# Smaller tiles (44 rows for 60), a smaller first tile and an unaligned TensorE program in a channel-gate kernel

## The chip, the cores and the metric

One core of one Trainium2 chip. The metric is the device time of one execution in microseconds (us); lower is better.

## The reference

```python
def reference(x, w1d):                     # x: (1, 384, 384, 384) bf16, w1d: (1,) bf16
    B, H, W, C = x.shape
    g = jnp.einsum("bhwc->bc", x) / (H * W)     # mean of each channel over all pixels
    s = _sigmoid(g * w1d[0])                    # (the loop over k = 1 taps, shortened)
    return x * s[:, None, None, :]
```

The input is 113.25 MB and so is the output. The kernel treats x as 1152 rows: one row is 128 pixels, one on each of 128 partitions, of 384 channels (768 bytes on each partition).

## The kernel before

Read literally, the reference needs two passes over x: one for the mean and one for the product. The kernel makes a single pass by a guess. It computes the gate `s_early` from the first few rows only, multiplies every tile by it in place and stores the tile. Meanwhile TensorE sums all rows. At the end the true gate `s_true` is computed and compared bit by bit in bf16. If any channel differed, a second pass would redo everything. With this input the gates agree, so the second pass is only a flag that is read and found to be zero.

```python
FIRST, TILE, PART, SLOTS = 12, 60, 28, 4
...
def sum_others():
    def one(e, s):                                   # one tile, in slot s
        e.wait_ge(ready, 1).then_inc(ready, -1)
        for r, n in parts:                           # parts = (0, PART), (PART, TILE-PART)
            add_rows(e, 1, (slot(s) + r) * C, n, 0, False, False).then_inc(...)
    def emit(e):
        ...
        with e.Fori(0, rounds) as k:                 # TensorE's loop: one round is SLOTS tiles
            for s in range(some):
                one(e, s)
            if some < SLOTS:
                with e.If(k < rounds - 1):
                    for s in range(some, SLOTS):
                        one(e, s)
...
for k in range(n_tiles):
    if k >= SLOTS:
        j = k - SLOTS
        put(row0(j), slot(j), slot(j), TILE, parts)  # VectorE: two gates; ScalarE's queue: store
        if k < last:
            load(slot(k), TILE, row0(k))             # SyncE's queue: waits for that store
        else:
            for r, n in parts:                       # the last tile is loaded in two parts
                load(slot(k), TILE, row0(k), r, n)
    for r, n in parts:
        plan.relay(ready, "gpsimd", "tensor",        # tells TensorE that the tile has landed
                   rows(slot(k), TILE) if r == 0 else (), ...)
...
# the end: add the PSUM banks (VectorE), s_true (ScalarE), compare, reduce, flag (VectorE)
def second_pass(name, e):
    e.wait_ge(*checked)
    flag = e.value_load(redo[0:1, 0:1], min_val=0, max_val=1)
    with e.If(flag > 0):
        ...
@block.scalar
def _(e):
    plan.emit("scalar", e)
    second_pass("scalar", e)
    for token in plan.final:                         # all stores
        e.wait_ge(*token)
@block.tensor
def _(e):
    e.addr_align(256, max_nops=0)
    plan.emit("tensor", e)
```

A tile in slot `s` is loaded, summed, gated part by part, stored, and then the slot is loaded anew. The loop of TensorE is unrolled over four slots of 45 matmuls of 512 columns.

## Time and profile before

| | kernel before |
|---|---|
| time, median of 3 runs | 531.79 us (531.5 to 532.03) |
| span of the profiled run | 530.1 us |
| time per tile in mid-run (load + store of 11.80 MB) | 27.18 us, so 434 GB/s |
| last load landed, slowest DMA engine | 508.94 us |
| flag read by ScalarE | 526.81 us |
| last store landed: median of the 16 DMA engines / slowest one | 526.48 / 529.63 us |

The first view is the page of the kernel before: span, busy time of each engine, the DMA share in 40 slices (tenths, 9 is 90% or more), and the queues with packets, MB and share of the 16 engines' span.

```profile
span 530.1 us, 1079 instructions
...
PE 227.4 (43%) x857; PEld 0.2 (0%) x2; DVE 241.5 (46%) x57; ACT 2.7 (1%) x4; POOL 0.3 (0%) x6
...
DMA  8999999999999999999999999999999999999996
...
q10 hardware_dynamic: 3314, 121.90, 53.2%
q1 hardware_dynamic: 2880, 104.60, 45.9%
q8 instruction: 1, 0.02, 0.0%
q14 instruction: 2, 0.02, 0.0%
...
```

SyncE's queue q1 and ScalarE's queue q10 together fill 99.1% of the 16 engines' span, and no compute engine comes near (VectorE 46%, TensorE 43%). The line q8, of the kind "instruction", is a single packet of 16384 B, called the instruction fetch in this document. The trace's DMA records put it at 2.4 us, and it took 2.045 us. It is the only one of the run, though TensorE's loop goes through five rounds.

Two waits look large. The table of waits (engine and line, what was waited for, us in total, times, longest):

```profile
...
PE acc L236 <- PEq L275: 283.6, 18, 31.1
DVE arena L199 <- PE acc L236: 245.3, 16, 28.5
...
```

These are engines waiting for tiles that have yet to land. With the queues at 99.1% of the 16 DMA engines' span, none of this waiting lengthens the middle of the run.

Whether it stays full in the middle is read from the loads that SyncE issues (start, duration, count), in the timeline from 210 to 300 us:

```profile
...
213.45 81.87 SPq L109 DMA_DIRECT2D arena<-in_x_dram  x4
```

Four issues, the first start to the last end 81.87 us, one issue 0.33 us: three periods of 27.18 us. A data packet of 46080 B takes 1.702 us in the DMA records. A tile is 128 of them in and 128 out, so by even division 8 in and 8 out for each of 16 DMA engines, and 16 × 1.702 = 27.23 us, the period: the engines run without a gap.

So only start and end are left to gain. The end in the timeline (start us, duration, engine, line, operation, count, idle time before and its releaser):

```profile
...
508.96 6.56 DVE L199 TENSOR_TENSOR arena<-arena,s_early 128x12288 bf16<-128x12288 bf16 x1 [16.54 <-DMA arena<-in_x_dram]
509.08 12.30 PE L236 MATMUL acc<-arena,ones 128*128 128x512 bf16 x45 [31.13 <-PEq L275]
...
521.22 0.81 PE L236 MATMUL acc<-zeros,ones 128*128 128x512 bf16 x3
522.07 2.70 DVE L309 TENSOR_TENSOR total<-total,acc 128x384 f32<-128x384 f32 x6 [6.55 <-PE acc L236]
524.80 0.61 ACT L412 ACTIVATE s_true<-total,w_scaled 128x384 bf16<-128x384 f32 x1 [507.61 <-DVE total L309]
...
526.63 0.15 DVE L434 CAST redo<-wrong 128x1 int32<-128x1 f32 x1
```

The last load's slowest part lands at 508.94. Then two things race: the last gate and its store, and TensorE's sum of the whole last tile (13 us) with a chain of small steps to the flag. How the DMA drains, by stretch (window, its length, then busy time and instruction count of each engine, granted clock, DMA share, GB/s):

```profile
...
core 0: us, PE busy (x) PEld busy (x) DVE busy (x) ACT busy (x) POOL busy (x), PEclk, DMA share, GB/s
...
520.00:524.00 4.00, 2.03 (x10) 0.00 (x0) 1.79 (x5) 0.00 (x0) 0.00 (x0) 1.00 1.02 439
524.00:526.00 2.00, 0.00 (x0) 0.00 (x0) 1.28 (x3) 0.61 (x1) 0.00 (x0) 0.57 0.77 332
526.00:528.00 2.00, 0.00 (x0) 0.00 (x0) 0.71 (x3) 0.00 (x0) 0.00 (x0) 0.50 0.12 49
528.00:530.00 2.00, 0.00 (x0) 0.00 (x0) 0.00 (x0) 0.00 (x0) 0.00 (x0) 0.50 0.09 33
...
```

From 526 us on the DMA share is about a tenth, which is one or two of the 16 engines: 14 have finished by 527.05, and two land their part of the last store at 529.34 and 529.63. ScalarE's last store wait passes at 529.65 and the span ends 0.45 us later. The slowest DMA engine sets the end.

### The profile page before, as it was taken

To read this page: it belongs to the slowest core of one execution; us is meant where nothing else is said; L and a number is where in the kernel's file an instruction comes from. 1 tells how busy PE (TensorE), PEld (TensorE's weight loads), DVE (VectorE), ACT (ScalarE), POOL (GpSimd) and SP (SyncE) were. 2 spreads that over 40 slices of the span, in tenths; PEclk is the share of its full clock that TensorE was granted. 3 is DMA by queue.
4 is the path that set the end of the run, shared out by engine and by line. 5 is a ranking of instruction groups with operands and counts; after the bars stand their busy time and mean duration, and the time that the engine had idled before them with its cause. 6 is when DMAs were issued, how large, how long until landed. Compare 5 with 4: busy or idle time off the path is not lost. (4 is left out here: it accounts for less than half of the span.)

```text
span 530.1 us, 1079 instructions
## 1 busy us (share of the span) xinstructions
PE 227.4 (43%) x857; PEld 0.2 (0%) x2; DVE 241.5 (46%) x57; ACT 2.7 (1%) x4; POOL 0.3 (0%) x6
## 2 busy tenths in 40 slices
PE   2284971052434436262717080908080808070053
PEld 0000000000000000000000000000000000000000
DVE  0353997008080907172625353445344443538142
ACT  1000000000000000000000000000000000000000
POOL 0000000000000000000000000000000000000000
PEclk9786987568686958585858585859686868777567
DMA  8999999999999999999999999999999999999996
GB/s 361 445 445 404 408 445 438 421 431 435 445 428 428 431 435 445 431 424 435 435 445 431 424 428 442 445 428 428 428 442 445 424 431 424 445 420 458 418 421 299
DMA packets 6197, 226.53 MB, mean 427 GB/s; under 512 B 690, under 2 KB 690, under 8 KB 690
## 3 DMA queue, kind: packets, MB, share of 16 engines
q10 hardware_dynamic: 3314, 121.90, 53.2%
q1 hardware_dynamic: 2880, 104.60, 45.9%
q8 instruction: 1, 0.02, 0.0%
q14 instruction: 2, 0.02, 0.0%
HBM read 113.25 MB, written 113.25 MB: 427 GB/s over the span
## 5 line engine op out<-in xcount | busy, mean ns | idle before, releaser
L199 DVE TENSOR_TENSOR arena<-arena,s_early 128x10752 bf16<-128x10752 bf16 (+2 forms) x39 | 234.8, 6063 | 264.2 <-PE acc L236 245.3
L236 PE MATMUL acc<-arena,ones 128*128 128x512 bf16 x849 | 224.9, 429 | 285.0 <-PEq L275 283.6
L309 DVE TENSOR_TENSOR total<-total,acc 128x128 f32<-128x128 f32 (+2 forms) x11 | 4.5, 409 | 6.9 <-PE acc L236 6.5
L307 DVE COPY total<-acc 128x384 f32<-128x384 f32 x1 | 0.6, 558 | 11.4 <-PE acc L236 11.4
L234 PE MATMUL acc<-arena,ones 128*128 128x512 bf16 x1 | 0.6, 606 | 7.6 <-DMA arena<-in_x_dram 7.6
L412 ACT ACTIVATE s_true<-total,w_scaled 128x384 bf16<-128x384 f32 x1 | 0.6, 614 | 507.6 <-DVE total L309 507.6
L236 PE MATMUL acc<-zeros,ones 128*128 128x512 bf16 x6 | 2.3, 505 | 0.0
L338 ACT ACT_TABLE_LOAD x1 | 1.3, 1283 | 2.2 <-issue 2.2
L344 PE MATMUL w_all<-w_one,ones 1*128 1x1 bf16 x1 | 0.2, 158 | 2.0 <-DMA w_one<-in_w1d_dram 2.0
L420 DVE TENSOR_TENSOR total<-s_true,s_early 128x384 f32<-128x384 uint16 x1 | 0.6, 559 | 0.7 <-ACT s_true L412 0.7
L353 DVE TENSOR_SCALAR w_scaled<-w_all 128x1 f32<-128x1 f32 x2 | 0.2, 154 | 1.3 <-PE w_all L344 1.3
L375 ACT ACTIVATE s_early<-total,w_scaled 128x384 bf16<-128x384 f32 x1 | 0.6, 614 | 12.9 <-DVE total L309 12.9
L428 DVE TENSOR_REDUCE wrong<-total 128x1 f32<-128x384 f32 x1 | 0.6, 553 | 0.0
L362 DVE MEMSET ones<- 128x128 bf16 x1 | 0.2, 165 | 0.8 <-PEq L512 0.8
L338 ACT ACTIVATE warm<-warm 128x1 f32<-128x1 f32 x1 | 0.2, 203 | 0.0
L434 DVE CAST redo<-wrong 128x1 int32<-128x1 f32 x1 | 0.2, 153 | 0.0
L234 PEld LDWEIGHTS acc<-arena,ones 128*128 128x128 bf16 x1 | 0.1, 105 | 7.7 <-DMA arena<-in_x_dram 7.7
L344 PEld LDWEIGHTS w_all<-w_one,ones 1*128 1x128 bf16 x1 | 0.1, 101 | 2.0 <-issue 2.0
L512 POOL MEMSET const-bfloat16-1.0<- 128x1 bf16 x1 | 0.1, 101 | 0.0
L512 POOL MEMSET const-uint8-127<- 128x1 uint8 x1 | 0.1, 101 | 0.0
L361 POOL MEMSET zeros<- 128x2 bf16 x1 | 0.1, 99 | 0.0
L360 POOL MEMSET warm<- 128x1 f32 x1 | 0.1, 98 | 0.3 <-POOLq L512 0.3
(2 smaller groups left out, 0.2 us busy)
## 6 DMA issues: line engine op xcount, KB each, us to landing
out_dram<-arena ACTq DMA_DIRECT2D x18, 5760.0 KB, 53.5
arena<-in_x_dram SPq DMA_DIRECT2D x16, 5760.0 KB, 35.4
arena<-in_x_dram SPq DMA_DIRECT2D x2, 3072.0 KB, 37.3
arena<-in_x_dram ACTq DMA_DIRECT2D x1, 5760.0 KB, 45.1
out_dram<-arena ACTq DMA_DIRECT2D x1, 3072.0 KB, 14.1
arena<-in_x_dram ACTq DMA_DIRECT2D x1, 2688.0 KB, 18.7
arena<-in_x_dram SPq DMA_DIRECT2D x1, 2688.0 KB, 28.5
out_dram<-arena ACTq DMA_DIRECT2D x1, 2688.0 KB, 29.9
```

The source lines that it names most:

```text
L199: return lambda e: e.tensor_tensor(to_v, v, s_b, ALU.mult)
L234: loaded.append(e.matmul(bank, weights, moving, start=start, stop=stop))
L236: return e.add_instruction(mybir.InstMatmult(name=nc.get_next_instruction_name(), engine=mybir.EngineType.PE, ins=[e.lower_ap(moving), e.l ...
L307: emit = lambda e, part=part, of=of: e.tensor_copy(part, of)
L309: emit = lambda e, part=part, of=of: e.tensor_tensor(part, part, of, ALU.add)
L338: lambda e: e.activation(warm[:, 1:2], warm[:, 0:1], ACT_F.Sigmoid),
L344: lambda e: e.matmul(w_all[:, 0:1], ones[0:1, :], w_one[0:1, 0:1], start=True, stop=True),
L353: lambda e, i=i, n=n: e.tensor_scalar_mul(w_scaled[:, i : i + 1], w_all[:, 0:1], 1.0 / float(P * n)),
L375: lambda e: e.activation(s_early[:], total[:], ACT_F.Sigmoid, scale=w_scaled[:, 0:1]),
L412: lambda e: e.activation(s_true[:], total[:], ACT_F.Sigmoid, scale=w_scaled[:, 1:2]),
L420: lambda e: e.tensor_tensor(total[:], s_true[:].bitcast(U16), s_early[:].bitcast(U16), ALU.not_equal),
L428: lambda e: e.reduce_max(wrong[:], total[:], axis=mybir.AxisListType.X),
```

## The change

The intent of the change: tiles of 44 rows in four slots and a first tile of 8, so that TensorE's whole program is 160 instructions, and no alignment of that program. That a program of this length does without the alignment was an assumption; E2 puts the alignment back. Since 1152 = 8 + 26 × 44, there are 26 tiles instead of 19. More semaphores go with more DMAs. The texts below also count TensorE's program in "listed rows", the loop's body counted once: 204 before and 152 after by the prediction's count.

```diff
-FIRST, TILE, PART, SLOTS = 12, 60, 28, 4
+FIRST, TILE, PART, SLOTS = 8, 44, 20, 4
@@
-    plan = Planner(nc, "a", 50)
+    plan = Planner(nc, "a", 70)
@@
         @block.tensor
         def _(e):
-            e.addr_align(256, max_nops=0)
             plan.emit("tensor", e)
```

## The prediction

> **What bounds the kernel now.** The 16 DMA engines. The page's queue table gives 53.2% + 45.9% = 99.1% of the 16 engines' span; VectorE is busy 46%, TensorE 43%. In the middle a tile's load is issued every 27.23 us (timeline of SyncE: 213.45, 240.60, 267.83); a tile is loaded and stored, 11.80 MB, so 433 GB/s. [...] a packet of 46080 B takes 1.702 us, and 16 of them (8 in, 8 out on each engine) make 27.23 us, no gap. 226.5 MB at that rate are 523 us; about 7 us of the 530.1 us span are start, end and skew.
>
> The long idle times (TensorE 283.6 us, VectorE 245.3 us in the table of waits) are waiting for data and cost nothing. In the last 4 us the DMA share is about a tenth: one or two engines run 3 us behind the other fourteen. One cause is visible: a 16 KB instruction fetch of 2.045 us on one engine, 2.4 us after the start, when loads have just begun. [...]
>
> **What the change does.**
> - Same bytes, in packets of 33792 B instead of 46080. From two packet times (9216 B 0.347 us, 46080 B 1.702 us) a packet costs 0.008 us plus bytes at 27.2 GB/s, so 33792 B take about 1.250 us, a tile period 20.0 us. More packets and semaphore writes add about +1.0 us per engine, all on the critical path.
> - Buffers fall from 252 to 184 rows, but load, sum, gate and store shrink together: sum plus gates about 18 of a 109 us slot cycle before, about 13.5 of 80 after. I expect no starvation.
> - TensorE's program shrinks from 204 to 152 listed rows, unaligned. [...] If the fetch goes away (60%), its engine gains 2 us and the end skew shrinks: 0 to -2 us, as the second late engine stays.
> - Earlier first gate and store: worth nothing, as loads saturate the DMA anyway.
> - End: the last tile's sum falls from 13.0 to about 9.5 us, the last gate from 6.6 to 4.9, but the stores left after the last load shrink from 20.7 to about 15 us. The fixed chain after the sum (bank adds 2.7 us, sigmoid, comparison, flag read, store waits: about 7 us) doesn't shrink. Today the stores end about 1 us after it; after the change it may end last: 0 to +2 us.
>
> **Sum.** 531.8 + 1.0 - 1 (fetch) + 0.7 (end chain) = 532.5, say 532.3 us; range 529.0 to 535.5. Faster by over 2%: 1%; within 2%: 96%; slower: 3%.
>
> **What would show it.** SyncE's issues 20.0 us apart in mid-run at about 433 GB/s; queue shares still about 99%; no 16 KB fetch during the run; less straggling in the last 4 us; ScalarE's final waits for stores already satisfied when the flag has been read.
>
> **What would make it wrong.** A fetch per loop round on one engine (up to 7 × 2 us of lag: slower); DMA gaps because loads wait for stores; address strides of 33 KB slowing the packets; the second late engine having the same cause as the first (faster, about 529).

No term of the sum is cut: 531.8 + 1.0 - 1 + 0.7 = 532.5. The 60% behind the fetch's -1 us was the author's estimate; of the fetch itself the trace shows the single 16384 B packet of 2.045 us. That an engine once behind stays behind was not shown in this form: in the kernel before the slowest engine was 3.80 us behind the median one at the first load, 6.5 to 6.7 us at the stores in mid-run and 3.15 us at the last store.

## The result

| | before | after |
|---|---|---|
| median of 4 runs each | 531.91 us (531.5 to 532.04) | 532.45 us (531.73 to 533.47) |
| ratio after / before | | 1.0013, 95% interval 0.9991 to 1.0034 |
| span of the profiled run | 530.1 us | 529.9 us |
| 16 KB fetch on a DMA engine | at 2.4 us, 2.045 us long | none |
| last load landed, slowest engine | 508.94 us | 512.04 us |
| flag read by ScalarE (start of the read) | 526.81 us | 527.27 us |
| last store landed: median / slowest engine | 526.48 / 529.63 us | 526.83 / 528.47 us |

A ratio here is the mean time of one kernel's runs over that of the other's runs of the same rounds, so it is not quite the ratio of the medians quoted. The profiled run of after is one of its two quicker ones (531.73 us); the other two took 533.11 and 533.47. All outputs are right.

The page of the kernel after, the same lines. There is no q8 line any more:

```profile
span 529.9 us, 1133 instructions
...
PE 242.0 (46%) x858; PEld 0.2 (0%) x2; DVE 243.1 (46%) x71; ACT 2.7 (1%) x4; POOL 0.3 (0%) x6
...
DMA  8999999999999999999999999999999999999997
...
q10 hardware_dynamic: 4322, 119.54, 52.3%
q1 hardware_dynamic: 3888, 106.96, 47.1%
q14 instruction: 2, 0.02, 0.0%
...
```

The two large waits (table of waits) have not changed in kind:

```profile
...
PE acc L236 <- PEq L275: 262.4, 23, 23.7
DVE arena L199 <- PE acc L236: 258.0, 23, 20.5
...
```

The loads in mid-run (timeline, the same window). Five issues in 80.19 us make four periods of 19.97 us, 433 GB/s. A data packet of 33792 B takes 1.251 us in the DMA records (predicted 1.250), so the 33 KB strides did not slow the packets. The DMA is as full as before, 52.3% + 47.1% = 99.4%:

```profile
...
214.55 80.19 SPq L109 DMA_DIRECT2D arena<-in_x_dram  x5
```

The end in the timeline:

```profile
...
512.07 4.96 DVE L199 TENSOR_TENSOR arena<-arena,s_early 128x9216 bf16<-128x9216 bf16 x1 [11.28 <-DMA arena<-in_x_dram]
512.19 2.72 PE L236 MATMUL acc<-arena,ones 128*128 128x512 bf16 x6 [20.75 <-PEq L275]
515.13 6.72 PE L236 MATMUL acc<-arena,ones 128*128 128x512 bf16 x26 [0.22 <-issue]
521.68 0.81 PE L236 MATMUL acc<-zeros,ones 128*128 128x512 bf16 x3
522.53 2.69 DVE L309 TENSOR_TENSOR total<-total,acc 128x384 f32<-128x384 f32 x6 [5.50 <-PE acc L236]
525.26 0.61 ACT L412 ACTIVATE s_true<-total,w_scaled 128x384 bf16<-128x384 f32 x1 [513.94 <-DVE total L309]
...
527.08 0.15 DVE L434 CAST redo<-wrong 128x1 int32<-128x1 f32 x1
```

The last load lands 3 us later than before, because less is left to store behind it: from there the median engine takes 14.8 us to its last store, against 17.5 before. The sum takes 10.3 us instead of 13.0, and the flag is cast at 527.08 instead of 526.63: later than before, although the last tile is smaller. The prediction had 9.5 us for the sum, which is 13.0 scaled by the rows. In both traces the granted clock (PEclk, as a share of TensorE's full clock) is 0.50 when the last sum starts and 1.00 only from 514.0 us on in before and 517.0 in after, 4.9 and 4.8 us after the start: this slow stretch did not shrink with the tile. The drain of the DMA, by stretch:

```profile
...
520.00:524.00 4.00, 2.49 (x12) 0.00 (x0) 1.36 (x4) 0.00 (x0) 0.00 (x0) 1.00 1.02 436
524.00:526.00 2.00, 0.00 (x0) 0.00 (x0) 1.25 (x4) 0.61 (x1) 0.00 (x0) 1.00 1.01 433
526.00:528.00 2.00, 0.00 (x0) 0.00 (x0) 1.17 (x3) 0.00 (x0) 0.00 (x0) 0.82 0.18 74
528.00:530.00 2.00, 0.00 (x0) 0.00 (x0) 0.00 (x0) 0.00 (x0) 0.00 (x0) 0.50 0.01 4
...
```

The last line shows the end of the straggling: a DMA share of 0.01 from 528 to 530 us, where it was 0.09. The stores are done at 528.47, and the span still ends at 529.9. ScalarE's records say why. It begins to read the flag at 527.27, and from 528.51 on it passes its 14 store waits one after another, 0.076 us apart, without stopping at any; the last passes at 529.5. (Most of these wait instructions name the semaphores of two stores: 14 for 28 stores. The kernel before, with 21 stores, had 10 of them behind the flag, so about 0.3 us of the longer chain comes from the number of stores.) **The end has changed hands: it is now the chain sum, bank adds, sigmoid, comparison, flag, store waits.**

### The profile page after: what moved, and what is told of

Same layout as the page of the kernel before. It is cut to its first block, busy times and chain, and to the rows that moved or that the text cites. A ratio compares the mean times of both kernels' runs of the same rounds, so it can differ in the third digit from the quotient of the medians.

```text
span 529.9 us, 1133 instructions
## 1 busy us (share of the span) xinstructions
PE 242.0 (46%) x858; PEld 0.2 (0%) x2; DVE 243.1 (46%) x71; ACT 2.7 (1%) x4; POOL 0.3 (0%) x6
## 3 DMA queue, kind: packets, MB, share of 16 engines
q10 hardware_dynamic: 4322, 119.54, 52.3%
q1 hardware_dynamic: 3888, 106.96, 47.1%
## 5 line engine op out<-in xcount | busy, mean ns | idle before, releaser
L236 PE MATMUL acc<-arena,ones 128*128 128x512 bf16 x850 | 239.9, 449 | 275.4 <-PEq L275 262.4
L199 DVE TENSOR_TENSOR arena<-arena,s_early 128x7680 bf16<-128x7680 bf16 (+2 forms) x53 | 236.4, 4501 | 270.0 <-PE acc L236 258.0
L234 PE MATMUL acc<-arena,ones 128*128 128x512 bf16 x1 | 0.6, 607 | 3.0 <-DMA arena<-in_x_dram 3.0
```

What stands on the lines that cost most here:

```text
L199: return lambda e: e.tensor_tensor(to_v, v, s_b, ALU.mult)
L234: loaded.append(e.matmul(bank, weights, moving, start=start, stop=stop))
L236: return e.add_instruction(mybir.InstMatmult(name=nc.get_next_instruction_name(), engine=mybir.EngineType.PE, ins=[e.lower_ap(moving), e.l ...
```

## The experiments

Theory A: (1) the end is the later of two things, the last store's slowest DMA engine plus about 0.45 us, or the flag read plus about 2.6 us; (2) the instruction fetch puts one DMA engine behind for the rest of the run; (3) the change took away the fetch and so moved the first end forward, but its closing chain then came last. Rival B: the bytes set the time, and fetch and ends do not matter. Rival C: the fetch comes from the program's length and not from the alignment.

All 12 runs in one table, with before and after. "Fetch" is the 16384 B packet: start and duration in us. The stores are the last store's landing, median and slowest engine. All are read from the trace of the profiled run. "Bound" is the larger of slowest store + 0.45 and flag + 2.6 (each fitted to the kernels before and after).

| kernel | fetch | flag read | last store med / slowest | bound | span | time, median |
|---|---|---|---|---|---|---|
| before | 2.4, 2.05 | 526.81 | 526.48 / 529.63 | 530.1 stores | 530.1 | 531.9 |
| after | none | 527.27 | 526.83 / 528.47 | 529.9 chain | 529.9 | 532.5 |
| E1 before, unaligned | 70.3, 0.93 | 521.88 | 526.35 / 528.00 | 528.5 stores | 528.5 | 530.85 |
| E2 after, aligned | 1.9, 1.14 | 529.44 | 527.07 / 528.38 | 532.0 chain | 532.1 | 533.68 |
| E3 after, sum by parts | none | 523.65 | 526.64 / 528.31 | 528.8 stores | 528.8 | 530.79 |
| E6 before, early waits | 2.0, 1.80 | 524.47 | 526.31 / 528.76 | 529.2 stores | 529.2 | 531.46 |
| E8 after, again | none | 527.13 | 526.86 / 528.57 | 529.7 chain | 529.8 | 532.66 |
| E5 after, early waits | none | 527.31 | 526.68 / 527.97 | (see E5) | 529.0 | 531.86 |
| E7 tiles of 20 | 520.9, 1.05 | 527.89 | 529.68 / 531.32 | 531.8 stores | 531.8 | 534.18 |
| E9 three slots of 60 | none | 520.72 | 531.02 / 531.91 | 532.4 stores | 532.4 | 535.87 |
| E10 as E1 | 70.5, 0.93 | 523.88 | 526.44 / 529.21 | 529.7 stores | 529.7 | 531.08 |
| E11 as E3 | none | 524.58 | 526.76 / 528.37 | 528.8 stores | 528.9 | 530.85 |
| E4 E1 + sum by parts | 70.4, 0.93 | 520.30 | 526.36 / 528.92 | 529.4 stores | 529.4 | 531.46 |
| E12 E2 + sum by parts | 1.9, 1.20 | 524.90 | 526.85 / 528.77 | 529.2 stores | 529.3 | 531.29 |

Outside E5, whose edit changes the second term itself, the simple bound meets every span within about 0.1 us. That is the main support for part (1).

E1, E2, E3 and E6 shared one chip, then E8, E5, E7 and E9, then E10, E11 and E4, and last E12. On these four chips the kernel before had medians of 531.44, 531.67, 532.10 and 531.69 us. A profile shows one run: that of E1 is the quickest of its six, that of E10, the same kernel, the slowest of its six, so single spans are good for seeing which end came last, and the medians for the size.

### E1: the kernel before without the alignment

```diff
-            e.addr_align(256, max_nops=0)
             plan.emit("tensor", e)
```

> Kernel before, only the alignment of TensorE's program taken away (tiles of 60 stay). Theory A (the 16 KB fetch at the start delays one DMA engine for the whole run, and the alignment causes that fetch): no 16384 B packet, the last store lands about 2 us earlier than before's 529.7, and the last load's slowest engine about 2 us earlier than 508.9, so the span is about 528, ratio 0.996. Rival B (skew and fetch don't matter, the bytes alone set the time): ratio 1.000, last store still at 529.7. Rival C (the fetch comes from the program's length of over 200 instructions, not from the alignment): the 16384 B packet stays, or comes more than once, ratio 1.000 or more.

Measured: 530.85 us (530.26 to 531.93), ratio 0.998, interval 0.9936 to 1.0024. The times alone do not show a gain, since the kernel before scattered from 529.91 to 536.61 on that chip. The queue lines of the page still show the fetch:

```profile
...
q8 instruction: 1, 0.02, 0.0%
...
```

In the DMA records it lies at 70.3 us, when TensorE is about to go on to the fourth tile of the first round, and takes 0.93 us. So rival C is half right: with 204 listed rows aligned or 203 unaligned the fetch comes, while the unaligned programs of 152 and 158 rows (after, E9) have none. Without the alignment the fetch only comes later, at 70.3 us instead of 2.4. The last load's slowest part lands early, so the sum starts at 504.60 instead of 509.08 and the flag is cast at 521.70 (the timeline near the end):

```profile
...
504.60 11.86 PE L236 MATMUL acc<-arena,ones 128*128 128x512 bf16 x45 [29.04 <-PEq L275]
...
521.70 0.15 DVE L434 CAST redo<-wrong 128x1 int32<-128x1 f32 x1
```

Both ends come earlier, the stores by 1.6 us, and the stores still are the end. That the alignment caused the fetch was wrong; that the alignment made it hit at the very start was right.

### E2: the kernel after with the alignment

```diff
+            e.addr_align(256, max_nops=0)
             plan.emit("tensor", e)
```

> Kernel after, with the alignment put back (tiles of 44 stay). Theory A: the 16384 B fetch is back, one or two engines end about 3 us late, last store about 531 instead of 528.4, ratio to before about 1.003 to 1.005, about 2 us above after. Rival B: nothing changes against after, about 1.001. Rival C: no fetch, as the program is short; as after.

Measured: 533.68 us (532.26 to 533.95), ratio 1.0023, below the 1.003 to 1.005 expected, interval 0.9979 to 1.0067; the after of another chip had 1.0012 (E8). The fetch is back at 1.9 us, so for a short program the alignment does cause it. But the expected late store did not come: the last store's slowest engine landed at 528.38, as in after. The last load landed late instead. From the timeline near the end:

```profile
...
514.39 4.96 DVE L199 TENSOR_TENSOR arena<-arena,s_early 128x9216 bf16<-128x9216 bf16 x1 [11.12 <-DMA arena<-in_x_dram]
514.51 2.72 PE L236 MATMUL acc<-arena,ones 128*128 128x512 bf16 x6 [20.91 <-PEq L275]
...
529.25 0.15 DVE L434 CAST redo<-wrong 128x1 int32<-128x1 f32 x1
```

The last gate and the last sum start at 514.39 and 514.51, against 512.07 and 512.19 in after: 2.3 us later, and the whole closing chain with them. That the fetch made this load late is not shown: the profile is of a run of 533.9 us, that of after is of one of its quick runs, no slow run of after was profiled, and E12 below has the same fetch without a late last load.

### E3: the kernel after, TensorE released part by part

```diff
-            e.wait_ge(ready, 1).then_inc(ready, -1)
             for r, n in parts:
+                e.wait_ge(ready, 1).then_inc(ready, -1)
                 add_rows(...)
@@
             plan.relay(ready, "gpsimd", "tensor",
-                rows(slot(k), TILE) if r == 0 else (),
+                rows(slot(k) + r, n),
```

The last tile is loaded in two parts, but the kernel before and the kernel after both begin its sum only when both have landed. Here the first part is summed when it lands.

> Kernel after, with TensorE released for each part of a tile, not only when both parts of the last tile have landed: the final sum has 18 matmuls after the last load instead of 33. Theory A (in the kernel after the closing chain sum, bank adds, sigmoid, comparison, flag ends last, about 1 us after the stores): the chain is 3 to 5 us shorter, the final store waits become the end, span about 1 us shorter than after: 528.9 against 529.9, ratio to before about 0.998. Rival B (the stores end last also there): same as after.

Measured: 530.79 us, and six runs within 0.24 us (530.66 to 530.90); ratio 0.9974, interval 0.9931 to 1.0017. The timeline near the end:

```profile
...
512.59 4.96 DVE L199 TENSOR_TENSOR arena<-arena,s_early 128x9216 bf16<-128x9216 bf16 x1 [10.71 <-DMA arena<-in_x_dram]
512.73 5.50 PE L236 MATMUL acc<-arena,ones 128*128 128x512 bf16 x18 [9.86 <-PEq L276]
...
523.47 0.15 DVE L434 CAST redo<-wrong 128x1 int32<-128x1 f32 x1
```

After the last load 18 matmuls are left instead of 33 (32 of which the trace of after recorded); the flag is cast at 523.47, 3.6 us earlier than in after. The span falls by 1.1 us and no further, because the stores now end at 528.31. Also the two groups of times that after shows (E8) are gone.

### E6: the kernel before, store waits ahead of the flag

```diff
+            for token in plan.final[:-2]:
+                e.wait_ge(*token)
             second_pass("scalar", e)
-            for token in plan.final:
+            for token in plan.final[-2:]:
                 e.wait_ge(*token)
```

> Kernel before, with ScalarE waiting for all stores but the last two before it reads the flag, not after. Theory A: before's end is the landing of its last store (529.65), which this doesn't touch: ratio 1.000, span 530.1 within 0.2. Rival (the closing chain is already the end in the kernel before): about 1 us shorter.

Measured: 531.46 us (531.01 to 531.65), the kernel before 531.44; ratio 0.9988, interval 0.993 to 1.0045. The times are equal, as expected. The span of the profiled run was 529.2, outside the 0.2 us expected; its last store happened to land at 528.76 (its fetch took 1.80 us), and the span followed the store by 0.45 us. The end is the store here too.

### E8: the kernel after, again

> The kernel after, unchanged, as the yardstick for the next runs and for the scatter: 532.5 us median as before, scatter over 531.7 to 533.5, no 16384 B packet, closing chain ends last (flag read about 527.3, stores landed about 528.5, span about 530).

Measured: 532.66 us, ratio 1.0012, interval 0.9995 to 1.003. Six runs in two groups: 531.53 and 531.59, then 532.35 to 533.18. The profile, again of a quick run, repeats the reading: no fetch, flag read 527.13, last store 528.57, span 529.8.

### E5: the kernel after, store waits ahead of the flag

The edit is that of E6.

> Kernel after, with ScalarE waiting for all stores but the last two before it reads the flag. Theory A (in the kernel after, the closing chain ends last, and its last piece is the row of about 14 store waits, 1 us, after the flag): the span ends at the later of flag + 1.2 us and last store + 0.4 us, so about 0.8 us shorter than after, ratio to after about 0.9985, and after minus this is close to what E3 gained. Rival B (stores end last): same as after. In the kernel before the same edit left the last store as the end (E6).

Measured: 531.86 us (530.78 to 532.10), ratio 0.9997 against E8's 1.0012 on the same chip: 0.8 us less by the medians, and the spans differ by 0.8 us (529.0 against 529.8). The last store landed at 527.97, so stores alone would have allowed 528.4; the end is the flag plus 1.7 us, not 1.2 as expected, since about 0.5 us pass between the branch on the flag and the first wait behind it. Thus an edit that touches neither a matmul nor a byte gains 0.8 us in the kernel after and nothing measurable in the kernel before (E6). The intervals of the two ratios, 0.9982 to 1.0013 and 0.9995 to 1.003 (E8), overlap a little; the reading rests on the traces as much as on the times.

### E7: tiles of 20 rows in 12 slots

```diff
-FIRST, TILE, PART, SLOTS = 12, 60, 28, 4
+FIRST, TILE, PART, SLOTS = 12, 20, 8, 12
-    plan = Planner(nc, "a", 50)
+    plan = Planner(nc, "a", 70)
-            e.addr_align(256, max_nops=0)
```

> Kernel before without alignment (as E1, same TensorE program), but 57 tiles of 20 rows in 12 slots instead of 19 of 60 in 4: same bytes, same buffer, three times as many packets, of 15360 B. It multiplies the packet cost by itself: 608 more packets per engine at 0.008 us each and 76 more semaphore writes at 0.009 us make about +5.5 us against E1, so about 536 us, ratio to before about 1.008; the change itself (208 more packets) would then owe about 1.8 us of packet cost at most, and by the sum of packet times about 1.1. Rival (packet count is free, bytes alone count): same as E1, 531 us.

Measured: 534.18 us (533.72 to 534.48), ratio 1.0043, interval 1.0023 to 1.0063. The packet cost is real but smaller than expected. The sum of the packet times per engine rose by 5.1 us against E1, or 5.8 with the semaphore writes (worked out: 5.5), but the median engine's last store landed only 3.33 us later (529.68 against 526.35): neighbouring packets overlap a little in the records (between 120 and 480 us they add up to 1.0021 of the elapsed time in E1 and 1.0070 in E7), so a sum of packet times counts too much. The rise in the end is 3.33 us for 608 packets and 76 semaphore writes, 4.9 ns each, with packets of 15 to 46 KB. The expectation also had a slip: the change adds 112 packets per engine (416 instead of 304), not 208. At 4.9 ns, with its 14 more semaphore writes, that would be 0.6 us (an estimate from this run).

### E9: three slots of 60 rows

```diff
-FIRST, TILE, PART, SLOTS = 12, 60, 28, 4
+FIRST, TILE, PART, SLOTS = 12, 60, 28, 3
```

With E1's and E3's edits (no alignment, sum by parts) and 70 semaphores. It was to combine large packets with a program of 158 listed rows.

> Tiles of 60 in three slots without alignment, TensorE released by parts: 158 listed rows of program instead of 152 and 192 buffered rows instead of 184, so the large packets of before with the short program of after. Theory A: no 16 KB fetch, closing chain off the end, about 1 us less packet cost than E3: stores end about 527.5, span about 528, ratio to before 0.995 to 0.997. Rival (three slots starve the DMA): loads are issued more than 27.4 us apart, DMA share below 98%, 535 us or more.

Measured: 535.87 us (534.18 to 541.33), ratio 1.0113, interval 1.0072 to 1.0154. There is no 16 KB fetch, so the short program does what it should; yet this is the slowest kernel of all, and the rival holds. The stretches from 56 to 72 us (columns as above):

```profile
...
56.00:60.00 4.00, 3.95 (x19) 0.00 (x0) 4.00 (x2) 0.00 (x0) 0.00 (x0) 1.00 0.96 415
60.00:64.00 4.00, 4.00 (x20) 0.00 (x0) 4.00 (x2) 0.00 (x0) 0.00 (x0) 1.00 0.75 323
64.00:68.00 4.00, 4.00 (x20) 0.00 (x0) 4.00 (x2) 0.00 (x0) 0.00 (x0) 1.00 0.64 196
68.00:72.00 4.00, 1.14 (x6) 0.00 (x0) 4.00 (x1) 0.00 (x0) 0.00 (x0) 0.99 1.10 357
...
```

The DMA share falls to 0.75 and 0.64, with 323 and 196 GB/s. In the timeline from 50 to 70 us SyncE issues a single load, at 64.72:

```profile
...
64.72 0.33 SPq L109 DMA_DIRECT2D arena<-in_x_dram  x1
```

The first three tiles had all landed by then. The fourth tile's load waits until the first tile's store has landed (at 64.7 us), and meanwhile the next gated tile is not ready: both queues run dry. Later the DMA is full again. The median engine's last store is 4.6 us later than in E10 or E4. The buffer of 192 rows is larger than the 184 of the kernel after, which does not starve; what is missing is the fourth slot.

### E10, E11 and E4: the candidates on one chip

E10 is E1 again, E11 is E3 again, E4 is E1 with E3's edit.

> E1 again, beside E11 and E4 on one chip, as the runs of the kernel before scattered over 529.9 to 536.6 in the first round. Theory A: last store about 528.0, flag read about 522, span 528.5, ratio to before 0.996 to 0.998. Rival B (the alignment doesn't matter): 1.000.

> E3 again on the same chip as E10. Theory A: closing chain about 4 us ahead of the last store, span about 528.8, ratio to before 0.997 to 0.998, with narrow scatter (530.66 to 530.9 before), as the end no longer hangs on the final sum. Rival (tiles of 44 cost a measurable 1 us of packets against tiles of 60): 1 us above E10.

> E1 plus TensorE released by parts. Theory A: in E1 the flag is already read some 6 us before the last store lands, so a shorter closing chain gives nothing: same as E10 within 0.3 us, the flag about 526 or earlier, the last store about 528. Rival (the parts release is worth about 1 us wherever it stands, for instance because buffers come free earlier): 1 us below E10.

Measured: E10 531.08 us (529.96 to 531.52), ratio 0.9967, interval 0.9938 to 0.9996. E11 530.85 us (530.68 to 531.24), ratio 0.9967, interval 0.9939 to 0.9995. E4 531.46 us (530.87 to 531.84), ratio 0.9979, interval 0.995 to 1.0007. E4 gains nothing over E10 (its median is 0.4 us higher; within 0.3 was expected), because in E1 and E10 the flag is read 5 to 6 us before the last store has landed. Tiles of 44 cost no measurable 1 us against tiles of 60: the median engine's last store is 0.3 to 0.4 us later in E11 than in E10 and E4. The slowest engine is 2.6 to 2.8 us behind the median in E4 and E10, which have the fetch at 70 us, and 1.6 us in E11, which has none; in E1 it was 1.64. E10 is the same kernel as E1, but its last load landed at 506.83 and not at 504.45, and its last store at 529.21, where 528.0 was expected. So a difference of 1 to 2 us between two single profiles is within the scatter.

E1 and E3 in both their runs, and E4 and E12, have lower medians than the kernel before on the same chip, by 0.4 (E12) to 1.25 us (E11), and than the kernel after. The gain is in the typical run: the kernel before had single runs of 533 to 536 us on E10's chip, which help these ratios, while by the lowest runs the gap is 0.2 us there for E11 and 0.9 for E10 (530.85 before, 530.68 and 529.96), and on the chip of E1 and E3 the lowest run of the kernel before, 529.91, is below all of theirs.

### E12: E2 with the sum by parts

> E2 (tiles of 44, alignment put back, 16384 B fetch at the start) plus TensorE released by parts. In E2 the last store landed no later than in the kernel after (528.4), but the last load 2.3 us later, and the closing chain behind it set the end. Theory A2 (the fetch hurts tiles of 44 only through the last load and the chain): with the chain shortened by 4 us the span is 529 to 529.5, ratio to before 0.997 to 0.998, about 2.5 us below E2, and close to E3. Theory A as first put (the fetch also makes the last store late): last store about 531, ratio 1.000 or more.

Measured: 531.29 us (530.97 to 531.69), ratio 0.9997, interval 0.9983 to 1.0011: the expected 0.997 to 0.998 was missed. The span is 529.3, 2.8 us below E2, with the same early fetch (1.9 us, 1.20 us long), and the last store lands at 528.77 and not at 531. From the timeline near the end:

```profile
...
512.93 4.96 DVE L199 TENSOR_TENSOR arena<-arena,s_early 128x9216 bf16<-128x9216 bf16 x1 [11.31 <-DMA arena<-in_x_dram]
...
524.72 0.15 DVE L434 CAST redo<-wrong 128x1 int32<-128x1 f32 x1
```

The last gate starts 1.5 us earlier than in E2 (514.39), and no later than in E11, which has no fetch (513.20). So 1.5 us of the 4.5 by which the flag is cast earlier than in E2 are not owed to the release by parts, and E12 does not test theory A2: the late last load, through which the fetch was to hurt, did not come. What an early fetch costs with tiles of 44 stays open; the spans of E12 and E11, on different chips, differ by 0.4 us.

## Why the prediction was right

The predicted 532.3 us met the measured 532.45, and its statement that nothing would move by over 2% held. Point by point:

- **The DMA bounds the kernel, and smaller tiles do not starve it: right.** The period is 19.97 us for 8.65 MB (predicted 20.0), 433 GB/s, and the queue shares are 52.3% + 47.1% (predicted about 99%). E9 shows that this was not to be had by the number of buffered rows: three slots with more rows starved.
- **The fetch vanishes, 0 to -2 us, mean -1: right in the result.** The last store's slowest engine landed 1.2 us earlier (528.47 against 529.63), as its lag behind the median engine fell from 3.15 to 1.65 us. That one engine falls behind with the fetch is shown. The very first load lands 3.80 and 2.63 us behind the median engine on its slowest one in before and E6, 1.30 and 1.44 in E2 and E12, and 0.2 to 1.0 in the profiles with no fetch by then. In mid-run (200 to 440 us) a tile's store in before still lands 6.5 to 6.7 us behind on its slowest engine, 1.1 to 1.2 on the next; with tiles of 44 and no fetch it is 1.0 to 2.6 on the slowest. That the fetch also sets the end is not shown, for two reasons. First, in before a second engine lands its last store only 0.29 us ahead of the slowest (529.34), whereas the fetch is one packet and the lag in mid-run was on one engine (6.5 us against 1.1 on the next). Had this second engine stayed, as the prediction assumed, the missing fetch could have gained 0.29 us; but in after the second engine lands at 527.82, 1.0 us behind the median instead of 2.9. Second, the change with the fetch put back (E2, E12) lands its last store at 528.38 and 528.77, hardly later than without (527.97 to 528.57 in after, E3, E5, E8 and E11). So the smaller tiles may have taken away the lag as well as the missing fetch, and this stays open.
- **More packets, +1.0 us: too large.** The median engine's last store moved by 0.35 us (526.48 to 526.83). Part of the error was to take the sum of recorded packet times for elapsed time; by E7 a packet cost about 4.9 ns and not 8. By the pace of the load issues in mid-run (27.20 us for 60 rows over 11 periods, 19.97 us for 44 over 17) the whole run would be 0.8 us longer (an estimate), so some 0.4 us may have been won back at the start or the end; this was not looked into.
- **The closing chain ends last, 0 to +2 us, mean +0.7: right.** In the profiled run it ended 1.0 us after what the stores alone would have allowed (528.47 + 0.45 = 528.9, against 529.9). E3 and E5 take away parts of it by quite different edits and gain 1.1 and 0.8 us of span; E6 gains nothing in the kernel before.
- **What was only luck in the size:** the packet term was 0.65 us too large, and it is open whether the stores' end moved for the predicted reason. In the profiled run the terms are +0.35 (packets), -1.5 (lag) and +1.0 (chain), together -0.15, and the span fell by 0.2. The median of the times rose by 0.5 all the same, because after has slower runs of 533 us which no profile caught. Their absence in E3 and E11 fits a closing chain that sometimes starts later, as E2's does, but that is argued, not shown.

So the fetch went, as intended, and the time did not fall: what the stores' earlier end gained was given back within the same 2 us, by a chain that until then had hidden behind two slow DMA engines. The version that keeps the gain is E3 (E11): the change plus the release by parts. The kernel before with only the alignment taken away (E10) is as fast on the same chip, 531.08 us against 530.85.

## What to carry to other kernels

Here the DMA engines were full (queue shares of 99.1% before and 99.4% after), and outside E5 every profiled run ended at the later of two things, the slowest DMA engine (plus 0.45 us) and the compute that must follow the last load (flag read plus 2.6 us); write both down with their times before shortening one, since the gain is capped by the distance to the other. The smaller last tile shortened its own sum from 13.0 to 10.3 us, but it also left fewer stores behind the last load (17.5 to 14.8 us to the median engine's last store), so the closing chain behind that sum moved to the end. When buffers are cut, count slots in the start-up phase and not rows alone: four slots of 44 rows kept the DMA full (99.4% over the run) where three of 60 did not (a DMA share of 0.64 from 64 to 68 us).
